# Block 0 of a retention-and-FFN kernel: fewer half steps, another order in the fifth visit, a step kept for chunk 8

## The chip, the cores and the metric

The kernel runs on one core of one Trainium2 chip. Its engines are named as the profile names them: PE (TensorE, matmuls; PEld is its weight load), DVE (VectorE), ACT (ScalarE), POOL (GpSimd) and SP (SyncE, which issues most transfers). The metric is the device time of one execution in microseconds (us); lower is better.

## The reference

Eight heads of retention over eight sequences of 576 tokens, and then a feed-forward layer with squared ReLU over all 4608 tokens:

```python
# q, k, v: (8, 8, 576, 64)
scores = (1 / sqrt(D)) * q @ k.T
ret = scores * Dmat            # Dmat[h, i, j] = gamma_h ** (i - j) for i >= j, else 0
attn = ret @ v
x = attn.transpose(0, 2, 1, 3).reshape(4608, 512)
h = np.maximum(x @ w_in, 0.0)  # w_in: (512, 2048)
out = h * h @ w_out            # w_out: (2048, 512)
```

## The kernel before

The retention runs in chunks of 128 tokens (five to a sequence, the last of 64). The feed-forward layer runs in blocks of 512 tokens, and each product of a block is a *step* on a list, which the loop over the chunks takes from to fill PE between the small matmuls of retention. Blocks 1 to 8 use products of sums and differences of quarter matrices (lines 595 and 866); block 0 uses plain products, because its weights are still being brought in.

The weights arrive as raw 64-bit words and are converted to float32 in 16 *pieces* for `w_in`, each by five DVE and two ACT operations. `round_parts` gives the six parts, and `w_in_parts` deals them out in order. `convert(n)` emits the next n of them:

```python
# lines 196 to 230, shortened
def fetch_w(j):
    if j < len(pieces) and wide:
        nc.sync.dma_start(raw_of(j)..., piece_src(j))            # L196
...
    def one():    nc.vector.tensor_scalar(exp, hi, ...)          # L210, waits for the raw piece
    def two():    nc.vector.tensor_scalar(bits, hi, ...)         # L214
    def beside():
        nc.scalar.activation(exp, exp, ...)                      # L218
        nc.scalar.activation(frac, lo, ...)                      # L219
    def three():  nc.vector.scalar_tensor_tensor(t, bits, ...)   # L222
    def four():   nc.vector.tensor_tensor(t, t, exp, ...)        # L225
    def five():   nc.vector.scalar_tensor_tensor(bits, hi, ...)  # L228
```

```python
    def w_in_parts():

        parts = [round_parts(j) for j in range(N_W1)] + [[None] * 2]
        for j in range(N_W1):
            one, two, beside, three, four, five = parts[j]
            if j <= N_HALF:
                yield from (one, two)
            yield beside
            if j >= N_HALF:
                yield from parts[j + 1][0:2]
            yield three
            yield four

            def last(five=five):
                five()
                n_made[0] += 1
                if n_next[0]:
                    fetch_raw(2)

            yield last
```

So from piece `N_HALF` on, the first two parts of the next piece come before the last three of a piece.

One piece's product for block 0 is `first_in(j)`: 512 tokens at once, or 256 of them (`halves`) when the block's other tokens aren't there yet. Its result is squared later, from a queue that the next calls empty:

```python
def first_in(j, halves=(0, 1)):
    assert n_made[0] > j
    ...
    for c in range(N_DM):
        nc.tensor.matmul(p..., lhsT=w[:, c, :], rhs=xT[0][:, c, lo * HT:hi * HT], ...)   # L559
    ...
    nc.scalar.activation(t, p, AF.Relu)                                                  # L564
    some(2)
    queue.append(lambda: nc.vector.tensor_tensor(t, t, t, op=ALU.mult))                  # L567
```

Of a chunk, `turn(i)` transposes k and q on PE (L387), copies kT on ACT (L393) and makes qT on DVE (L395, or L397 with the decay from chunk 4 on); `scores(i)` needs both (L415) and masks the result on DVE (L420 or L422). `retain_a` and `retain_c` add the chunk's own products and grow the state (L436, L439), `retain_b` adds the state's part (L471) and ends with a small ACT copy that serves as a fence for what follows on PE:

```python
    nc.scalar.copy(u_sb[...][:, 0:2, 0:1], xp[0][:, :, cs - CH:cs - CH + 1])             # L474
```

`retain_c` then copies the chunk's result to the block's xT on ACT (L493). The steps of block 0, and what takes them from chunk 4 on:

```python
    def block_steps(n):
        if n == 0:
            seconds = [(0, lambda j: (first_in(j, (1,)), first_in(j + 1, (1,))), j) for j in range(0, N_HALF, 2)]
            return seconds + [(0, first_in, j) for j in range(N_HALF, N_W1)]
        return [(n, ffn_in, n, mp, j) for mp in range(N_MP) for j in range(NP)]
...
    N_0 = N_W1 - N_HALF // 2
    PACE = (...)          # points (tokens, steps done) that the later visits aim at
...
    def ffn(i, half):

        gone[0] += chunks[max(0, min(i, N_CH - 1))][3] / 2
        if steps and steps[0][0] == 0:

            for f in (step, lambda: convert(6)) if half else (lambda: convert(6), step):
                f()
            if half and steps and steps[0][0] == 0:
                step()
                convert(6)
            return
        ...
```

The loop's visits; i counts from 0, `N_EARLY` is 4, so visit 4 is the fifth:

```python
    for i in range(N_CH + 1):
        if i <= N_EARLY:

            if i == 1:
                convert(2)
            elif i == 2:
                convert(5)
            if i >= 1:
                retain_a(i - 1)
                if i < 3:
                    warm(4, False)
                else:
                    convert(1)
                    first_in(2 * i - 5, (0,))
                    convert(5)
                retain_b(i - 1)
                if i < 3:
                    warm(4, False)
                retain_c(i - 1)
            convert((0, 1, 1, 0, 1)[i])
            if i == N_EARLY:
                fetch_raw(2)
                step()
            scores(i)
            if i == 2:
                convert(5)
                first_in(0, (0,))
            elif i == 3:
                convert(1)
                first_in(2, (0,))
                convert(5)
            elif i == N_EARLY:
                convert(5)
                step()
                convert(6)
            if i < N_EARLY:
                if i + 1 < N_EARLY:
                    scale_q(i + 1, nc.gpsimd)
                if i < 2:
                    warm(6, False)
                turn(i + 1)
        else:
            if i == N_EARLY + 1:
                gone[0] = TOK
            retain_a(i - 1)
            if i < N_CH:
                turn(i)
            ffn(i - 1, 0)
            retain_b(i - 1)
            if i < N_CH:
                scores(i)
            retain_c(i - 1)
            ffn(i - 1, 1)
        if i == 0:
            fetch_raw(2)
        if i + 3 < N_CH:
            load(i + 3)
        if 0 < i < N_EARLY:
            fetch_raw(1)
    assert n_next[0] == N_BLK
```

Of the kernel before, what the change touches and what calls it, by code (L numbers as in the profile page):

```python
# [40 lines left out]
def kernel(  # L41
# [87 lines left out]
    N_EARLY = TOK // C  # L129
# [27 lines left out]
    pieces = [(0, m, e) for m in range(N_M) for e in range(2)]  # L157
    pieces += [(1, mq + mh * N_MQ, e) for mq in range(N_MQ) for mh in range(2) for e in range(2)]
    N_W1 = N_DF
    N_HALF = 4  # L160
    stage = [W[5].rearrange("p (o s f) -> p o s f", o=4, s=NP),
             W[6][:, 0:3 * NP * 128].rearrange("p (o s f) -> p o s f", o=3, s=NP)]
    N_RAW = 6
# [30 lines left out]
    def fetch_w(j):  # L194
        if j < len(pieces) and wide:
            nc.sync.dma_start(raw_of(j).bitcast(I64).rearrange("p (c f) -> p c f", c=N_DM), piece_src(j))  # L196
# [88 lines left out]
    def fetch_raw(count):  # L285

        for _ in range(count):
            if n_raw[0] < min(N_W1, n_made[0] + N_RAW):
                fetch_w(n_raw[0])
                n_raw[0] += 1  # L290

    def w_in_parts():

        parts = [round_parts(j) for j in range(N_W1)] + [[None] * 2]
        for j in range(N_W1):
            one, two, beside, three, four, five = parts[j]
            if j <= N_HALF:
                yield from (one, two)
            yield beside  # L300
            if j >= N_HALF:
                yield from parts[j + 1][0:2]
            yield three
            yield four
# [9 lines that stand above are left out]
    w_in_steps = w_in_parts()  # L314

    def convert(count):
        for _ in range(count):
            f = next(w_in_steps, None)
            f and f()
# [39 lines left out]
    def rows(half, n=64):  # L359
        return slice(64 * half, 64 * half + n)  # L360
# [13 lines left out]
    def scale_q(i, engine):  # L374

        ci, t = chunks[i][1], loaded[i][0]
        engine.tensor_tensor(t, t, dv[:, :, NCH + ci:NCH + ci + 1].to_broadcast([C, H, D]), op=ALU.mult)

    def turn(i):

        cs, c0 = chunks[i][3], chunks[i][2]
        n_h = cs // CH
        p = ps_t.tile([128, 2, 512], F32, tag="t", name="t_ps").rearrange("p h (j d t) -> p h j d t", j=2, d=HP)
        for j in (1, 0):
            for hp in range(HP):
                for h in range(n_h):
                    nc.tensor.transpose(p[:, h, j, hp, :], loaded[i][j][rows(h), 2 * hp:2 * hp + 2, :],  # L387
                                        ident[rows(h), rows(h)])
        for j, name in ((1, "kT"), (0, "qT")):
            t = st[i][name] = work2.tile([128, HP, C], F32, tag=name, name=name) if j == 0 else work.tile([128, HP, C], F32, tag=name, name=name)  # L390
            to = t[:, :, :cs].rearrange("p d (h t) -> p h d t", h=n_h)
            if j:
                nc.scalar.copy(to, p[:, :n_h, j, :, :])  # L393
            elif i < N_EARLY:
                nc.vector.tensor_copy(to, p[:, :n_h, j, :, :])  # L395
            else:
                nc.vector.tensor_tensor(to, p[:, :n_h, j, :, :], dq[:, :, c0:c0 + cs].rearrange("p d (h t) -> p h d t", h=n_h),  # L397
                                        op=ALU.mult)
# [145 lines left out]
    def some(count=1):  # L544
        for f in queue[:count]:
            f and f()
        del queue[:count]

    def first_in(j, halves=(0, 1)):

        assert n_made[0] > j
        wi, m, e = pieces[j]
        mp, mm = divmod(m, 2)
        p = ps_f.tile([128, 2, HT], F32, tag="f", name="h_ps")
        w = w_in[mp][:, mm, 2 * e:2 * e + 2, :, :].rearrange("p s c f -> p (s c) f")
        lo, hi = halves[0], halves[-1] + 1
        p = p[:, lo:hi, :]
        for c in range(N_DM):
            nc.tensor.matmul(p.rearrange("p h t -> p (h t)"), lhsT=w[:, c, :], rhs=xT[0][:, c, lo * HT:hi * HT],  # L559
                             start=(c == 0), stop=(c == N_DM - 1))  # L560

        t = g_room[mp % 2][:, 3:7:3, mm, :] if e else g_room[mp % 2][:, 0:5:4, mm, :]
        t = t[:, lo:hi, :]
# [4 lines that stand above are left out]
        if mm and e and hi == 2:  # L568
            queue.append(lambda: [nc.sync.dma_start(
                g_dram[0, a:b, :, 2 * mp:2 * mp + 2, :].rearrange("s p m t -> p s (m t)"),  # L570
                g_room[mp % 2][:, a:b, :, :].rearrange("p s m t -> p s (m t)")) for a, b in QUARTERS])
        if j >= N_W1 - 4:

            sums_w.setdefault(0, sum_w_in(0)).pop(0)()
            if n_next[0] > 1:
                if 1 not in sums_x:
                    sums_x[1] = sum_x(1)
                sums_x[1].pop(0)()
# [73 lines left out]

    def block_steps(n):
        if n == 0:
            seconds = [(0, lambda j: (first_in(j, (1,)), first_in(j + 1, (1,))), j) for j in range(0, N_HALF, 2)]
            return seconds + [(0, first_in, j) for j in range(N_HALF, N_W1)]
        return [(n, ffn_in, n, mp, j) for mp in range(N_MP) for j in range(NP)]

    def step():
        n, f, *args = steps.pop(0)  # L660
        done[0] += 1
        f(*args)
# [3 lines left out]

    HALF = C // 2
    N_0 = N_W1 - N_HALF // 2
    PACE = ((4 * TOK + HALF // 4, N_0 + 2 * N_MP * NP - 2), (5 * TOK - HALF, N_0 + 3 * N_MP * NP - 2),  # L670
            (6 * TOK + HALF // 4, N_0 + 4 * N_MP * NP - 2), (8 * TOK + HALF // 4, N_0 + 6 * N_MP * NP - 2),
            (9 * TOK, N_0 + 7 * N_MP * NP - 2))
    done = [0]
# [30 lines left out]
    def warm(count, wide):  # L704
        t = ps_f.tile([128, 512], F32, tag="f", name="idle_ps")
        for _ in range(count):
            if wide:
                nc.tensor.matmul(t[:, 0:128], lhsT=idle, rhs=idle, start=True, stop=True)
            else:
                for b in range(2):  # L710
                    nc.tensor.matmul(t[rows(b), 0:64], lhsT=idle[rows(0), rows(b)], rhs=idle[rows(0), 0:64], start=True, stop=True,
                                     skip_group_check=True)
# [4 lines left out]
# [8 lines that stand above are left out]
                retain_a(i - 1)  # L725
                if i < 3:
                    warm(4, False)
                else:
                    convert(1)
                    first_in(2 * i - 5, (0,))  # L730
                    convert(5)
                retain_b(i - 1)
                if i < 3:
                    warm(4, False)
                retain_c(i - 1)
            convert((0, 1, 1, 0, 1)[i])
            if i == N_EARLY:
                fetch_raw(2)
                step()
            scores(i)  # L740
            if i == 2:
                convert(5)
# [3 lines that stand above are left out]
                first_in(2, (0,))  # L746
                convert(5)
            elif i == N_EARLY:
                convert(5)
                step()  # L750
                convert(6)
            if i < N_EARLY:
                if i + 1 < N_EARLY:
                    scale_q(i + 1, nc.gpsimd)
                if i < 2:
                    warm(6, False)
                turn(i + 1)
        else:
            if i == N_EARLY + 1:
                gone[0] = TOK  # L760
# [15 lines that stand above are left out]
# [239 lines left out]
```

## Time and profile before

| | before |
|---|---|
| device time, median of 3 runs | 993.59 us (993.35 to 995.42) |
| span of the profiled execution | 991.7 us |
| mean granted PE clock | 0.998 of full speed |
| DVE busy | 748.6 us (75%) |
| ACT busy | 190.4 us (19%) |
| transfers over the span | 221 GB/s |
| PE busy from 20 to 30, 30 to 40, 40 to 50 us | 7.83, 6.98, 9.32 us |
| PE busy from 50 to 100 us | 50.00 us |

The profile is one execution. An engine is busy while it works on an instruction; waiting is not busy. A matmul of float32 is recorded as two, so that `first_in` on half the tokens leaves 8 records of 128x256. A wait names the instruction that released it. An arrow in brackets after a row of the timeline shows how long the engine had been idle before it and who ended that. All the line numbers are those of the kernel before; in the changed kernel they are one higher from line 160 on and up to four higher near the end of the loop.

### The profile page before, as it was taken

To read this page: it belongs to the slowest core of one execution; us is meant where nothing else is said; L and a number is where in the kernel's file an instruction comes from. 1 tells how busy PE (TensorE), PEld (TensorE's weight loads), DVE (VectorE), ACT (ScalarE), POOL (GpSimd) and SP (SyncE) were. 2 spreads that over 40 slices of the span, in tenths; PEclk is the share of its full clock that TensorE was granted. 3 is DMA by queue.
4 is the path that set the end of the run, shared out by engine and by line. 5 is a ranking of instruction groups with operands and counts; after the bars stand their busy time and mean duration, and the time that the engine had idled before them with its cause. 6 is when DMAs were issued, how large, how long until landed. Compare 5 with 4: busy or idle time off the path is not lost.

```text
span 991.7 us, 24441 instructions
## 1 busy us (share of the span) xinstructions
PE 973.5 (98%) x10532; PEld 869.5 (88%) x10532; DVE 748.6 (75%) x1427; ACT 190.4 (19%) x462; POOL 81.6 (8%) x85
## 2 busy tenths in 40 slices
PE   7899999999999999999999999999999999999998
PEld 7655688888888888888888889999999999999998
DVE  4688696567878888897886777777777777777765
ACT  3444222222222222223221010000000000000000
POOL 3100011111111111111111000000000000000000
PEclk9999999999999999999999999999999999999999
DMA  9984657665696878769458999675673757556351
GB/s 205 250 239 143 174 172 208 162 175 176 187 311 199 223 234 260 224 209 283 142 212 297 404 389 348 235 283 163 230 268 148 265 197 270 192 213 216 126 212 44
DMA packets 187676, 220.40 MB, mean 222 GB/s; under 512 B 119216, under 2 KB 137648, under 8 KB 178608
## 3 DMA queue, kind: packets, MB, share of 16 engines
q1 hardware_dynamic: 185456, 218.31, 67.8%
q8 instruction: 83, 1.36, 0.6%
q10 hardware_dynamic: 2112, 0.52, 0.2%
q14 instruction: 25, 0.20, 0.1%
HBM read 129.41 MB, written 89.39 MB: 221 GB/s over the span
## 4 chain that ended last, share of the span: by engine, by line
PE 91%; DVE 5%; DMA 1%; SPq 1%; issue 1%; ACT 1%; DVEq 0%; ACTq 0%
PE o_b L866 17%; PE h_b L595 16%; PE o_c L866 11%; PE o_a L866 11%; PE h_a L595 10%; PE h_c L595 10%; PE h_ps L559 5%; PE x_ps L436 3%; PE t_ps L387 2%; PE sc_ps L415 2%; PE x_ps L471 2%; DVE room L602 1%; PE u_ps L439 1%; DMA w<-in_moe_w_in_dram 1%; DMA w<-in_moe_w_out_dram 0%
## 5 line engine op out<-in xcount | busy, mean ns | idle before, releaser
L595 PE MATMUL h_b<-room,w 128*128 128x256 f32 x736 | 177.2, 383 | 1.2 <-DVE room L520 0.9
L595 PEld LDWEIGHTS h_b<-room,w 128*128 128x128 f32 x736 | 137.2, 190 | 21.4 <-PE t_ps L387 1.1
L866 PE MATMUL o_b<-w,room 128*128 128x128 f32 x1168 | 144.5, 275 | 0.2 <-DVE room L817 0.2
L866 PEld LDWEIGHTS o_b<-w,room 128*128 128x128 f32 x1168 | 137.2, 192 | 0.5 <-DVE room L817 0.4
L866 PE MATMUL o_c<-w,room 128*128 128x128 f32 x1008 | 123.0, 275 | 0.0
L866 PEld LDWEIGHTS o_c<-w,room 128*128 128x128 f32 x1008 | 117.7, 192 | 0.0
L595 PE MATMUL h_c<-room,w 128*128 128x256 f32 x480 | 114.4, 381 | 0.0
L595 PE MATMUL h_a<-room,w 128*128 128x256 f32 x448 | 107.6, 383 | 0.0
L595 PEld LDWEIGHTS h_c<-room,w 128*128 128x128 f32 x480 | 90.4, 190 | 12.6
L595 PEld LDWEIGHTS h_a<-room,w 128*128 128x128 f32 x448 | 83.7, 190 | 11.8
L866 PE MATMUL o_a<-w,a 128*128 128x128 f32 x688 | 85.6, 275 | 0.0
L866 PEld LDWEIGHTS o_a<-w,a 128*128 128x128 f32 x688 | 81.2, 192 | 0.1
L612 POOL TENSOR_TENSOR room<-room 128x512 f32<-128x512 f32 x32 | 35.2, 1100 | 438.2 <-ACT room L611 370.6
L602 DVE SCALAR_TENSOR_TENSOR room<-room 128x512 f32<-128x512 f32 x96 | 68.1, 710 | 3.3
L880 ACT COPY r<-o_a 128x128 f32<-128x128 f32 x53 | 14.1, 266 | 271.7 <-PE o_a L866 241.2
L559 PE MATMUL h_ps<-room,w 128*128 128x512 f32 (+1 forms) x160 | 60.1, 526 | 2.5 <-DVE w L228 1.7
L614 DVE TENSOR_TENSOR room<-h_b,room 128x512 f32<-128x512 f32 x32 | 22.1, 690 | 46.9 <-PE h_b L595 46.9
L436 PEld LDWEIGHTS x_ps<-ret,v_ld 64*64 64x64 f32 x1152 | 40.4, 136 | 15.9 <-issue 11.7
L436 PE MATMUL x_ps<-ret,v_ld 64*64 64x64 f32 x1152 | 50.0, 226 | 3.5 <-ACT u_sb L474 3.4
L559 PEld LDWEIGHTS h_ps<-room,w 128*128 128x128 f32 x160 | 30.3, 196 | 24.6 <-issue 19.1
L424 POOL TENSOR_TENSOR v_ld<-v_ld,dv 128x512 f32<-128x512 f32 (+1 forms) x40 | 42.8, 1075 | 63.5 <-DMA v_ld<-in_v_dram 58.6
L876 DVE TENSOR_TENSOR small<-o_b,small 128x128 f32<-128x128 f32 x62 | 18.1, 292 | 38.4 <-PE o_b L866 38.4
(109 smaller groups left out, 1377.4 us busy)
## 6 DMA issues: line engine op xcount, KB each, us to landing
g_dram<-room SPq DMA_DIRECT2D x32, 1792.0 KB, 7.7
a<-g_dram SPq DMA_DIRECT2D x43, 1024.0 KB, 7.1
room<-g_dram SPq DMA_DIRECT2D x20, 1024.0 KB, 6.4
w<-w_dram SPq DMA_DIRECT2D x7, 1792.0 KB, 13.0
out_dram<-room SPq DMA_DIRECT2D x17, 512.0 KB, 3.4
w<-in_moe_w_in_dram SPq DMA_DIRECT2D x16, 512.0 KB, 6.1
w<-in_moe_w_out_dram SPq DMA_DIRECT2D x16, 512.0 KB, 4.1
v_ld<-in_v_dram SPq DMA_DIRECT2D x31, 256.0 KB, 4.4
```

The costliest lines, as they stand in the source:

```text
L387: nc.tensor.transpose(p[:, h, j, hp, :], loaded[i][j][rows(h), 2 * hp:2 * hp + 2, :], ident[rows(h), rows(h)])
L415: nc.tensor.matmul(sc[e][rows(h), hp, :], lhsT=kT[rows(e), hp, t], rhs=qT[rows(e), hp, t], start=True, stop=True, skip_group_check=True)
L424: nc.gpsimd.tensor_tensor(vs[:cs], vs[:cs], dv[:cs, :, ci:ci + 1].to_broadcast([cs, H, D]), op=ALU.mult)
L436: own.append(lambda hp=hp, e=e, b=b: nc.tensor.matmul(x_at(hp, b, h), lhsT=s["vs"][rows(h), 2 * hp + b, :], rhs=s["ret"][rows(h), e, hp, : ...
L471: nc.tensor.matmul(x_at(hp, b, h), lhsT=u[rows(e), hp, :], rhs=s["qT"][rows(e), hp, CH * h:CH * h + CH], start=clears(b, hp // 2), stop=Fa ...
L559: nc.tensor.matmul(p.rearrange("p h t -> p (h t)"), lhsT=w[:, c, :], rhs=xT[0][:, c, lo * HT:hi * HT], start=(c == 0), stop=(c == N_DM - 1))
L595: nc.tensor.matmul(p[:, mm, :], lhsT=w[:, c, :], rhs=xs[n][right][:, c, :], start=(j in OPENS and mm == 0 and c == 0), stop=(j in CLOSES a ...
L602: nc.vector.scalar_tensor_tensor(t, t, 0.0, t, op0=ALU.max, op1=ALU.mult)
L612: nc.gpsimd.tensor_tensor(g["A11"], g["A11"], g["A11"], op=ALU.mult)
L614: nc.vector.tensor_tensor(g["A22"], p, p15, op=ALU.add)
L866: nc.tensor.matmul(p, lhsT=s["lefts"][left][:, m, :], rhs=w_out[j][:, m, WO_SLOT[right], :], start=(i in OPENS and m == 0), stop=(i in CLO ...
L876: nc.vector.tensor_tensor(s["u2"], p, s["p1"], op=ALU.add)
```

## The change

The change touches block 0 only, while the weights of `w_in` arrive.

- `N_HALF` falls from 4 to 3: pieces 0 to 2 are done in two halves, piece 3 in one. The point from which the conversion deals parts of the next piece ahead stays at 4 (`N_ALONE`).
- The second halves become a step each instead of one step for two pieces, so block 0 has 16 steps and not 14.
- In visit 4 (the fifth), `turn(4)` moves from the end of visit 3 into the place between `retain_a` and `retain_b`. The conversion and the half product that stood there are gone, so no conversion stands in front of the fence at the end of `retain_b`; none stands between `retain_c` and `scores` either.
- `scores(4)` comes before the second halves, and two single steps with conversions follow it.
- With 16 steps, two in visit 4 and three in each of the next four, two steps are left for the visit of chunk 8, which had none of block 0 before.

The matmuls that are done are the same in sum. The whole diff:

```diff
--- before.py
+++ after.py
@@ -157,7 +157,8 @@
     pieces = [(0, m, e) for m in range(N_M) for e in range(2)]
     pieces += [(1, mq + mh * N_MQ, e) for mq in range(N_MQ) for mh in range(2) for e in range(2)]
     N_W1 = N_DF
-    N_HALF = 4
+    N_ALONE = 4
+    N_HALF = 3
     stage = [W[5].rearrange("p (o s f) -> p o s f", o=4, s=NP),
              W[6][:, 0:3 * NP * 128].rearrange("p (o s f) -> p o s f", o=3, s=NP)]
     N_RAW = 6
@@ -295,10 +296,10 @@
         parts = [round_parts(j) for j in range(N_W1)] + [[None] * 2]
         for j in range(N_W1):
             one, two, beside, three, four, five = parts[j]
-            if j <= N_HALF:
+            if j <= N_ALONE:
                 yield from (one, two)
             yield beside
-            if j >= N_HALF:
+            if j >= N_ALONE:
                 yield from parts[j + 1][0:2]
             yield three
             yield four
@@ -652,7 +653,7 @@
 
     def block_steps(n):
         if n == 0:
-            seconds = [(0, lambda j: (first_in(j, (1,)), first_in(j + 1, (1,))), j) for j in range(0, N_HALF, 2)]
+            seconds = [(0, first_in, j, (1,)) for j in range(N_HALF)]
             return seconds + [(0, first_in, j) for j in range(N_HALF, N_W1)]
         return [(n, ffn_in, n, mp, j) for mp in range(N_MP) for j in range(NP)]
 
@@ -666,7 +667,7 @@
 
 
     HALF = C // 2
-    N_0 = N_W1 - N_HALF // 2
+    N_0 = N_W1
     PACE = ((4 * TOK + HALF // 4, N_0 + 2 * N_MP * NP - 2), (5 * TOK - HALF, N_0 + 3 * N_MP * NP - 2),
             (6 * TOK + HALF // 4, N_0 + 4 * N_MP * NP - 2), (8 * TOK + HALF // 4, N_0 + 6 * N_MP * NP - 2),
             (9 * TOK, N_0 + 7 * N_MP * NP - 2))
@@ -725,18 +726,17 @@
                 retain_a(i - 1)
                 if i < 3:
                     warm(4, False)
+                elif i == N_EARLY:
+                    turn(i)
                 else:
                     convert(1)
-                    first_in(2 * i - 5, (0,))
+                    first_in(1, (0,))
                     convert(5)
                 retain_b(i - 1)
                 if i < 3:
                     warm(4, False)
                 retain_c(i - 1)
-            convert((0, 1, 1, 0, 1)[i])
-            if i == N_EARLY:
-                fetch_raw(2)
-                step()
+            convert((0, 1, 1, 0, 0)[i])
             scores(i)
             if i == 2:
                 convert(5)
@@ -746,15 +746,19 @@
                 first_in(2, (0,))
                 convert(5)
             elif i == N_EARLY:
-                convert(5)
-                step()
-                convert(6)
+                fetch_raw(2)
+                convert(1)
+                for _ in range(2):
+                    step()
+                    convert(5)
+                    convert(1)
             if i < N_EARLY:
                 if i + 1 < N_EARLY:
                     scale_q(i + 1, nc.gpsimd)
                 if i < 2:
                     warm(6, False)
-                turn(i + 1)
+                if i + 1 < N_EARLY:
+                    turn(i + 1)
         else:
             if i == N_EARLY + 1:
                 gone[0] = TOK
```

## The prediction

> **What bounds the kernel now.** First the page's busy table and slices, for the whole:
>
> ```profile
> PE 973.5 (98%) x10532; PEld 869.5 (88%) x10532; DVE 748.6 (75%) x1427; ACT 190.4 (19%) x462; POOL 81.6 (8%) x85
> ```
>
> TensorE (PE) is busy in 973.5 of 991.7 us, so 18 us at most can come from its idle time, and the diff neither adds nor removes matmul work. The change can only move idle time, and time at a lowered clock, in block 0. So next I read PE's list of waits for the first 115 us, and then the timeline around the largest.
>
> ```profile
> PE x_ps L436 <- ACT u_sb L474: 2.1, 2, 1.8
> PE h_ps L559 <- DVE w L228: 1.7, 3, 0.6
> PE h_ps L559 <- ACT room L493: 0.9, 2, 0.7
> PE sc_ps L415 <- DVE qT L397: 0.3, 1, 0.3
> ```
>
> The columns are total us, times, longest. The first line's 1.8 us is the fence of visit 4 (the fifth): PE waits for the small ACT copy L474. The timeline of PE, with start and duration first and the idle time in brackets, shows it and what follows it:
>
> ```profile
> 40.00 0.27 PE L436 MATMUL x_ps<-ret,v_ld 64*64 64x64 f32 x2 [1.80 <-ACT u_sb L474]
> ...
> 41.37 5.17 PE L559 MATMUL h_ps<-room,w 128*128 128x256 f32 x16 [0.68 <-ACT room L493]
> ...
> 47.08 3.72 PE L559 MATMUL h_ps<-room,w 128*128 128x256 f32 x16
> ...
> 55.45 0.69 PE L415 MATMUL sc_ps<-qT,kT 64*64 64x64 f32 x32
> ```
>
> The same 16 records (two half pieces) take 5.17 us and then 3.72 us: the first pair ran at a lowered clock. The windows view confirms it, its columns being PE, PEld, DVE, ACT and POOL busy, granted clock, DMA share, GB/s:
>
> ```profile
> 37.50:40.90 3.40, 1.39 (x65) 1.11 (x64) 1.43 (x4) 1.76 (x5) 0.00 (x0) 1.00 1.06 208
> 40.90:44.30 3.40, 2.93 (x7) 2.39 (x8) 0.00 (x0) 0.69 (x2) 1.06 (x1) 0.50 0.95 288
> ```
>
> Then what held ACT's copy. The timeline of DVE shows two long waits for raw weights, and the operation that scores of chunk 5 need:
>
> ```profile
> 37.90 0.43 DVE L210 TENSOR_SCALAR w<-w 128x512 uint32<-128x512 uint32 x1 [2.44 <-DMA w<-in_moe_w_in_dram]
> 38.24 0.42 DVE L214 TENSOR_SCALAR w<-w 128x512 uint32<-128x512 uint32 x1
> 38.57 0.42 DVE L397 TENSOR_TENSOR qT<-t_ps,dq 128x256 f32<-128x256 f32 x1
> 38.91 0.42 DVE L567 TENSOR_TENSOR room<-room 128x256 f32<-128x256 f32 x1
> 44.59 0.43 DVE L210 TENSOR_SCALAR w<-w 128x512 uint32<-128x512 uint32 x1 [5.26 <-DMA w<-in_moe_w_in_dram]
> ...
> 54.71 0.68 DVE L397 TENSOR_TENSOR qT<-t_ps,dq 128x512 f32<-128x512 f32 x1
> 55.31 0.42 DVE L210 TENSOR_SCALAR w<-w 128x512 uint32<-128x512 uint32 x1
> ```
>
> Raw piece 4 lands at 37.9 and raw piece 5 at 44.6. ACT's two conversion operations wait for DVE's L210 at 37.90, and the fence copy stands behind them on ACT. That is the 1.8 us. From 44.59 DVE runs without a gap until chunk 5's qT at 54.71, and PE asks for that qT at 55.45, just after it is ready.
>
> **What the Trainium skill says.** "TensorE: Matmul & The Clock Gate", Part 1: The HAM clock gate, says that PE is gated to half its clock after an idle window of about 3.4 us, in windows that run freely. The trace agrees in size: 3.4 us at clock 0.50 after a window with 1.39 us of PE work; so full idleness was not needed. "Perfetto Trace Analysis", Tensor Engine Instruction, says that ACT and DVE are strict FIFO; the L397 above that stands behind a waiting L210 agrees. The same page, Identifying the Most-Contended Engine, warns that PE's busy share doesn't measure the distance to its peak; the 2.93 busy us in a half-clock window show why I look at the clock too.
>
> **The change part by part.** A half piece costs 1.83 us at full clock (from 47.08 to 50.73 for two), a full piece 3.63 (51.38 to 55.01), so one full piece instead of two halves saves nothing. The parts differ in when things stand on each queue.
>
> *Removed in visit 4:* the conversion in front of the fence, and piece 3's first half (35.60 to 37.50). *Moved:* turn(4) comes after retain_a(3), the scores of chunk 4 before all second halves. *Left out there:* one of three whole conversions, and the work of pieces 3 and 4, which PE formerly did before scores(5).
>
> Fence: up to 33.65 nothing differs. retain_a(3) 0.70, turn(4) 0.64, retain_b(3) 0.69 and retain_c(3) 0.69, by the same rows of before, with two short waits on ACT copies, end at about 36.4; the 1.8 us wait is gone. But chunk 4's qT still stands behind piece 4's L210 and L214, issued on DVE in visit 3, and the SP order up to there is unchanged, so the raw piece still lands at 37.9: qT ends at 38.99, and scores(4) start at 39.05. PE idles some 2.6 us there.
>
> PE then has only scores(4) 0.61, three second halves 5.48, turn(5) 0.65 and retain_b(4) 0.44: 7.2 us, to about 46.2, before scores(5). Those need chunk 5's qT. DVE's queue before it now holds: from 44.59 (raw piece 5, again unchanged) the five operations of a conversion step to 47.32 as before; one square, 0.34; raw piece 6's two operations and piece 5's three, 2.72 (48.59 to 51.31 before); so qT starts at 50.38 and ends about 51.06. Raw piece 6 was issued at 39.67 and took 7.7 us in before, landing at 47.4, just in time. So scores(5) start at **51.1 instead of 55.45**, after some 5 us of PE idling.
>
> Balance at that point: 4.35 us earlier, but pieces 3 and 4 now lie ahead instead of behind, where before had done all four halves of them: 2 x 3.63 = 7.26 us. **Net loss 2.9 us.** The same from idle time: before loses 0.62 + 1.80 + 0.68 and 1.45 to the clock (5.10 less 3.65) between 33.65 and 55.45, 4.55 us; after loses 17.45 less 9.9 of work, 7.5 us.
>
> Clock: before paid 1.45 there. After, a stretch of 3 to 5 us without matmuls ends at 51.1, longer than the one that cost before its clock. A half clock for 3.4 us costs 1.7 us once PE is loaded again; I count **1.5**, between before's 1.45 and that, as windows may fall otherwise. A drop at 39 to 43 is hidden in the wait.
>
> From 51.1 to the end of visit 8 PE should be full, as it was from 47 to 104 before: DVE is one conversion further behind by visit but PE two pieces.
>
> Visit 9, chunk 8: two pieces remain (14 and 15) and stand in its two slots. Before, PE waited 0.30 us for qT of chunk 9 and then, in visit 10, for qT of chunk 10, which had five operations of block 1 in front of it:
>
> ```profile
> 122.85 0.69 PE L415 MATMUL sc_ps<-qT,kT 64*64 64x64 f32 x32 [1.48 <-DVE qT L397]
> ```
>
> After, chunk 10's qT stands behind one sum of block 1 only, and PE has three products between turn and scores: both waits go, **1.8 us gained**; block 1's second product may wait for its sum behind that qT, an estimate of 0.3 us from 0.6 us per operation there. Net -1.5.
>
> Sum: 2.9 + 1.5 - 1.5 = **+2.9**, from 993.6 to **996.5 us**. The pace afterwards aims at the same points, its count of steps raised by the same two, so the rest of the run should be alike.
>
> **Rivals.**
> 1. *The fence bounds the visit.* Then its 1.80, the 0.68 behind it and the 1.45 of clock are all saved and chunk 8's 1.5 too: some 988 to 989 us. For it: the wait list's first row and the chain, which goes through that fence. Against: the raw transfers at 37.9 and 44.6 stand behind every qT, and PE has little to do meanwhile.
> 2. *The clock doesn't drop, or a window falls well.* Then about 995.
> 3. *Raw piece 6 lands later or DVE becomes the bound through visits 5 to 8.* 7.7 us of flight ends only 0.3 us before it is needed; each us late is a us on scores(5). Then 998 to 1000. Against: DVE's busy share in 60 to 100 us was about 83% with PE full.
> 4. *Everything is hidden anyway.* With PE full for the remaining 900 us nothing absorbs a delay, so I give this little.
>
> **Range and chances.** 996.5, from 993.0 (half the conversion wait absorbed, no clock loss) to 1000.0 (two clock drops or a late transfer). 2% is 20 us, more than block 0's visit 4 can move: faster 0.005, same 0.985, slower 0.01.
>
> **What would show it.** Right: no L474 wait near 40; PE idle before scores(4) until 39.0, waiting for qT; a wait of 3 to 5 us before scores(5), ending at 51, for qT; half clock for some 3 us thereafter; no wait for qT at chunks 9 and 10. Wrong: scores(5) starting near 47, or raw pieces landing at other times, since all the times rest on those two landings.

## The result, and the profile after

The changed kernel takes 998.82 us (median of 4 runs, 998.12 to 1000.34); the kernel before, beside it, 994.2 us. The ratio is 1.0048, with a 95% interval of 1.003 to 1.0065: slower by some 4.6 us, within 2%. The profiled span grew from 991.7 to 996.4 us. Line numbers of the changed kernel are one higher here: L398 is the qT of L397, L475 the fence copy, L211 a conversion's first operation.

PE's waits of the changed kernel between 30 and 130 us (total us, times, longest):

```profile
PE sc_ps L416 <- DVE qT L398: 5.7, 2, 3.1
PE x_ps L437 <- ACT u_sb L475: 1.5, 3, 0.9
PE h_ps L560 <- DVE w L229: 0.5, 1, 0.5
```

The fence wait of 1.8 us near 40 is gone, though another fence wait of 0.9 us has come, and PE waits 5.7 us for qT, in two waits. The timeline of PE shows both, and the products behind them:

```profile
39.41 1.12 PE L416 MATMUL sc_ps<-qT,kT 64*64 64x64 f32 x16 [3.10 <-DVE qT L398]
40.46 5.54 PE L560 MATMUL h_ps<-room,w 128*128 128x256 f32 x16
...
51.55 1.13 PE L416 MATMUL sc_ps<-qT,kT 64*64 64x64 f32 x32 [2.59 <-DVE qT L398]
53.60 1.12 PE L437 MATMUL x_ps<-ret,v_ld 64*64 64x64 f32 x16 [0.92 <-ACT u_sb L475]
54.65 8.70 PE L560 MATMUL h_ps<-room,w 128*128 128x512 f32 x16
63.91 0.46 PE L388 MATMUL t_ps<-ident,k_ld 64*128 64x64 f32 x8
```

The scores of chunk 5 start at 51.55 (55.45 before). The two full pieces behind them, 3 and 4, take 8.70 us; before, two took 7.13 (the row at 56.53 further down). DVE's timeline says what these scores waited for:

```profile
38.26 0.43 DVE L211 TENSOR_SCALAR w<-w 128x512 uint32<-128x512 uint32 x1 [3.07 <-DMA w<-in_moe_w_in_dram]
...
45.02 0.43 DVE L211 TENSOR_SCALAR w<-w 128x512 uint32<-128x512 uint32 x1 [3.42 <-DMA w<-in_moe_w_in_dram]
...
50.81 0.68 DVE L398 TENSOR_TENSOR qT<-t_ps,dq 128x512 f32<-128x512 f32 x1
```

Raw pieces 4 and 5 land at 38.3 and 45.0 and DVE then runs without a gap to chunk 5's qT. The windows of the same profile show the clock (columns: PE, PEld, DVE, ACT, POOL busy, granted clock, DMA share, GB/s):

```profile
51.00:54.40 3.40, 1.93 (x47) 1.77 (x48) 3.33 (x7) 1.59 (x4) 0.00 (x0) 0.50 0.70 205
54.40:57.60 3.20, 3.20 (x11) 1.53 (x8) 3.13 (x8) 0.37 (x1) 0.00 (x0) 0.50 1.19 235
```

This half clock lasts from 51.0 to 57.8, 6.8 us: twice the 3.4 us that before had at 40.9 to 44.3. An earlier one, from 37.4 to 44.2, lies over the wait before the scores of chunk 4 and the two half pieces behind them (5.54 us).

### The profile page after: what moved, and what is told of

The parts are those of the page before. It is cut to its first block, busy times and chain, and to the rows that moved or that the text cites. A ratio compares the mean times of both kernels' runs of the same rounds, so it can differ in the third digit from the quotient of the medians. Undisturbed runs are those within 1.5% of the kernel's fastest.

```text
span 996.4 us, 24418 instructions
## 1 busy us (share of the span) xinstructions
PE 975.9 (98%) x10524; PEld 869.9 (87%) x10524; DVE 747.7 (75%) x1426; ACT 190.7 (19%) x461; POOL 83.9 (8%) x85
## 4 chain that ended last, share of the span: by engine, by line
PE 92%; DVE 4%; ACT 1%; DMA 1%; issue 1%; SPq 1%; DVEq 0%; ACTq 0%
PE o_b L870 17%; PE h_b L596 16%; PE o_c L870 11%; PE o_a L870 11%; PE h_c L596 11%; PE h_a L596 11%; PE h_ps L560 5%; PE x_ps L437 3%; PE t_ps L388 2%; PE x_ps L472 2%; PE sc_ps L416 2%; PE u_ps L440 1%; DMA w<-in_moe_w_in_dram 1%; PE idle_ps L712 0%; DVE room L603 0%
## 5 line engine op out<-in xcount | busy, mean ns | idle before, releaser
L560 PE MATMUL h_ps<-room,w 128*128 128x512 f32 (+1 forms) x152 | 62.1, 560 | 1.2 <-DVE w L229 1.0
L425 POOL TENSOR_TENSOR v_ld<-v_ld,dv 128x512 f32<-128x512 f32 (+1 forms) x40 | 44.2, 1108 | 69.2 <-DMA v_ld<-in_v_dram 47.6
L880 DVE TENSOR_TENSOR small<-o_b,small 128x128 f32<-128x128 f32 x62 | 18.1, 292 | 38.3 <-PE o_b L870 38.3
```

Of the source, the lines that this page charges most:

```text
L425: nc.gpsimd.tensor_tensor(vs[:cs], vs[:cs], dv[:cs, :, ci:ci + 1].to_broadcast([cs, H, D]), op=ALU.mult)
L880: nc.vector.tensor_tensor(s["u2"], p, s["p1"], op=ALU.add)
```

## The experiments

Each was timed beside the kernel before on the same chip. Its medians were 994.9 to 995.4 us there and 994.2 beside the changed kernel, so medians of two experiments can differ by about 1 us for that reason alone, and the ratio to before is the better measure. "Changed" is the kernel after, and scores(5) are the scores of chunk 5. The texts before each run call experiment 4 qt5_first, 5 qt5_fence and 11 both_qt. Diffs with comments in them are shortened.

**1. The fence alone.** In the kernel before, visit 4's conversion goes behind the fence.

```diff
-   convert(1); first_in(3, (0,)); convert(5)        # visit 4, before retain_b
+   first_in(3, (0,))
-   convert(1)                                       # visit 4, after retain_c
+   convert(7)
```

> The kernel before, with the conversion of piece 4 in visit 4 put behind the fence (nothing else moved). Theory (chunk 5's qT, behind three conversions on DVE that start when raw piece 5 lands near 44.6 us, sets when scores of chunk 5 start): the 1.8 us fence wait near 40 goes, but scores(5) still start near 55.4 and PE waits some 2 to 3 us for qT just before them; time within 1.5 us of before (about 994). Rival (the fence bounds the visit): the 1.8 us, the 0.7 us behind it and the 1.4 us of half clock are saved, about 990.5.

Measured: 996.14 us, ratio to before 1.0014 (1.0 to 1.0029). PE's timeline of this run:

```profile
39.30 0.27 PE L436 MATMUL x_ps<-ret,v_ld 64*64 64x64 f32 x2 [0.28 <-ACT u_sb L474]
...
56.67 0.80 PE L415 MATMUL sc_ps<-qT,kT 64*64 64x64 f32 x32 [1.99 <-DVE qT L397]
```

The fence wait fell from 1.80 to 0.28 us, and 1.99 us appeared before the scores of chunk 5. The half clock moved with the idle time, from 40.9 to 44.3 in before to 57.2 to 60.5 here, so that was not saved either. The fence wait was the longest in the visit and removing it gained nothing: some 16 us later PE can't pass chunk 5's qT in either kernel. Raw piece 5 landed at 45.81 in this profile, 1.2 us later than in before's, and the scores start as much later. The distance from this landing to scores(5) is 10.86 us in all three profiles with the old order: before (44.59 to 55.45), this one (45.81 to 56.67) and that of experiment 2 (45.02 to 55.88), while the fence wait is 1.80, 0.28 and 0.83 us. The fence, the longest wait that the change removed, was not the bound.

**2. The kept steps alone.** In the kernel before, chunks 6 and 7 take two steps, so that two are left for chunk 8.

```diff
-            if half and steps and steps[0][0] == 0:
+            if half and steps and steps[0][0] == 0 and i not in (N_EARLY + 2, N_EARLY + 3):
```

> The kernel before, with two full steps of block 0 kept for chunk 8 (the visits of chunks 6 and 7 take two steps and not three). Theory: the waits of 0.30 us (chunk 9's qT) and 1.48 us (chunk 10's qT) go and about 0.3 us comes back, so about 1.5 us faster than before, 992.7. Rival (the wait only moves to a later visit of block 1): the same as before, 994.2.

Measured: 992.88 us, ratio 0.9986 (0.997 to 1.0003). No wait of PE for another engine is listed between 100 and 130 us, where before had 1.8 us for qT. The interval includes 1. In its profile no half clock fell at 41 to 44, as before's did, but one at 22.5 to 25.9. So the waits are shown to be gone, and the gain in time is only likely.

**3. The changed kernel without the kept steps.**

```diff
                 step()
                 convert(6)
+                if i in (N_EARLY + 2, N_EARLY + 3):
+                    step()
+                    convert(6)
```

> The changed kernel without the two steps kept for chunk 8 (the visits of chunks 6 and 7 take four steps each). Theory: the waits for qT of chunks 9 and 10 come back, about 1.5 us slower than the changed kernel, 1000.3. Rival (the kept steps pay nothing here): 998.8.

Measured: 1000.71 us, ratio to before 1.006 (1.0045 to 1.0075), against 1.0048 of the changed kernel. Its waits between 100 and 130 us:

```profile
PE sc_ps L416 <- DVE qT L398: 1.8, 2, 1.5
```

The same 1.8 us as before are back. So the kept steps remove these waits in both kernels. In time they are worth 1.2 us here by the ratios, 1.9 by the medians; the intervals overlap, so the size is not shown.

**4. Chunk 5's qT first, fence as it was.** In the changed kernel, the last seven parts of visit 4 move to just behind turn(5).

```diff
-                for _ in range(2):
-                    step()
-                    convert(5)
-                    convert(1)
+                step()
+                convert(5)
+                step()
...
             if i < N_CH:
                 turn(i)
+            if i == N_EARLY + 1:
+                convert(7)
             ffn(i - 1, 0)
```

> The changed kernel with the last seven conversion parts of visit 4 moved to just behind turn(5), so that chunk 5's qT stands in front of piece 5's conversion on DVE, all conversions of visit 5 still in front of its fence. Theory (qT behind the conversion makes the wait, but the fence of visit 5 is a second bound at nearly the same time): scores(5) start near 49.3 and not 51.6, but PE then waits for the fence copy until about 53.5, and the time stays within 1 us of the changed kernel, 998.8. Rival (qT is the only bound there): 2.5 us of waiting and the half clock go, 993 to 995.

Measured: 998.47 us, ratio 1.0039 (1.0019 to 1.0058), as the changed kernel. PE:

```profile
50.82 0.69 PE L416 MATMUL sc_ps<-qT,kT 64*64 64x64 f32 x32 [1.20 <-DVE qT L398]
55.60 1.12 PE L437 MATMUL x_ps<-ret,v_ld 64*64 64x64 f32 x16 [4.09 <-ACT u_sb L475]
```

The wait for qT shrinks and the fence's grows to 4.09 us. The fence copy stood on ACT behind the conversions of pieces 5 to 7. Raw piece 5 landed at 47.01 here, 2.0 us later than in the changed kernel's profile, and this was the slowest of the four runs (1001.44), so the times are to be read from that landing: chunk 4's own products start 8.59 us behind it, in the changed kernel 8.58 (45.02 to 53.60). The move freed the scores and left the fence where it was.

**5. Both bounds at once.** As 4, but the seven parts and the conversion of visit 5's first half (six parts) go behind the scores of chunk 5 and the products of chunk 4.

```diff
+   # visit 5, behind turn(5): step(); retain_b(4); scores(5); retain_c(4)
+   convert(13)
```

> As qt5_first, but the moved conversion and that of the visit's first half stand behind the fence and the scores of chunk 5. Theory (both bounds gone): scores(5) near 49.3, no fence wait, clock full after 51, so pieces 3 and 4 take 7.3 us and not 8.7; about 5.5 us faster than the changed kernel, 993.3. Rival (PE then runs into unfinished conversions, because they start later): a new wait of PE for DVE at pieces 5 to 7, gain under 2 us, 997 or more.

Measured: 1000.16 us, ratio 1.0048 (1.0033 to 1.0063): no gain, and my theory's 5.5 us missed. Yet in visit 5 what it said happened, a little later:

```profile
50.38 0.65 PE L416 MATMUL sc_ps<-qT,kT 64*64 64x64 f32 x32
...
51.55 7.13 PE L560 MATMUL h_ps<-room,w 128*128 128x512 f32 x16
```

The scores started without a wait, and the two pieces ran at full clock. The waits between 56 and 72 us show where the gain went:

```profile
PE x_ps L437 <- ACT u_sb L475: 1.3, 1, 1.3
PE x_ps L472 <- ACT u_sb L446: 1.0, 1, 1.0
PE sc_ps L416 <- DVE qT L398: 1.0, 1, 1.0
```

Visit 6 now has 3.3 us of waits for the same three things, with half clock from 66 to 73 after them. The 13 parts that I moved stood in front of *chunk 6's* qT, kT and fence. The rival had the time right, but not the place: PE waited in visit 6, not at pieces 5 to 7.

**6. The same with fewer parts.** Only the count differs from 5: seven parts come later.

```diff
-                convert(13)
+                convert(6)
```

> As qt5_fence, but 6 parts of conversion and not 13 behind the scores of chunk 5, so that 7 parts fewer stand in front of chunk 6's qT on DVE; the rest follows later, as each visit deals out the same number. Theory (qt5_fence won 4.7 us by chunk 6's turn and lost it in visit 6, where chunk 6's qT and fence stood behind the conversions that it had moved there): the waits of 3.3 us in visit 6 and the half clock behind them go, and what qt5_fence was to bring comes, 993 to 995, so 4 to 6 us under the changed kernel. Rival (DVE has no room for them later either): the waits come back in visit 7 or 8, 998 or more.

Measured: 992.08 us (6 runs, 991.0 to 993.01), ratio 0.9965 (0.9949 to 0.9981). No wait of PE for another engine is listed from 56 to 75 us, and PE's timeline runs through:

```profile
48.22 0.69 PE L416 MATMUL sc_ps<-qT,kT 64*64 64x64 f32 x32 [1.17 <-DVE qT L398]
48.73 0.64 PE L437 MATMUL x_ps<-ret,v_ld 64*64 64x64 f32 x16
49.30 7.13 PE L560 MATMUL h_ps<-room,w 128*128 128x512 f32 x16
...
61.71 0.69 PE L416 MATMUL sc_ps<-qT,kT 64*64 64x64 f32 x32
```

Some 8 us under 5, by the place of seven parts on two queues. (Raw piece 5 landed at 44.41 here and at 45.96 in 5's profile; that accounts for 1.5 us between the two profiles at most.) It also shows that the changed kernel's other parts can beat the kernel before once the conversions stand elsewhere.

**7. The conversion in front of visit 5's fence alone.** The changed kernel with that one `convert(6)` behind `retain_c(4)`.

> The changed kernel with the one conversion in front of visit 5's fence put behind the scores of chunk 5 and chunk 4's own products. Theory (the fence copy stands on ACT behind the conversion of piece 7, whose first operation waits on DVE behind chunk 5's qT): the 0.9 us wait for the fence copy near 53 goes, the half clock stays; 0.5 to 1.5 us faster than the changed kernel, 997.3 to 998.3. Rival (the later conversion gives it back at chunk 6's qT, as when more conversions were moved): no difference.

Measured: 997.81 us, ratio 1.0021 (0.9994 to 1.0048). The 0.9 us wait went, the half clock stayed, from 50.3 to 57.2:

```profile
52.64 1.07 PE L437 MATMUL x_ps<-ret,v_ld 64*64 64x64 f32 x16
```

From the landing of raw piece 5 to the next turn PE took 17.89 us (45.20 to 63.09), 1.0 less than in the changed kernel (45.02 to 63.91). The medians also differ by 1.0 us and the ratios by 2.7, though the intervals overlap.

**8. Chunk 4's qT alone.** In the changed kernel, piece 4's first two parts move behind scores(4): `convert(5)` to `convert(3)` in visit 3, `convert(1)` to `convert(3)` in visit 4.

> The changed kernel with chunk 4's qT alone put in front of the two operations that wait for raw piece 4; those of piece 5 stay in front of chunk 5's qT. Theory (scores(5), bound by raw piece 5 and two conversion steps behind it, are the bound; the wait before scores(4) is only a part of the same waiting): scores(4) start near 36.5 and not 39.4, the wait before scores(5) grows by what was saved, to 5 us or more, scores(5) stay near 51.5; within 1.5 us of the changed kernel, 998.8. Rival (the two waits add up): 2.5 us faster, 996.3.

Measured: 998.72 us, ratio 1.0033 (1.0005 to 1.0061), the same as the changed kernel. PE:

```profile
51.46 0.95 PE L416 MATMUL sc_ps<-qT,kT 64*64 64x64 f32 x32 [4.48 <-DVE qT L398]
```

The wait of scores(4) for qT shrank from 3.10 to 0.19 us (0.70 us more stood idle inside these scores, with no releaser in the profile), and that before scores(5) grew from 2.59 to 4.48; they still start at 51.5. The first wait was part of the second. Scores(5) start 6.53 or 6.54 us behind the landing of raw piece 5 in all six profiles that have the changed kernel's conversions between the two: the changed kernel (45.02 to 51.55), 3, 7, 8, 9 and 10.

**9 and 10. Is the half clock a cost of its own?** Small matmuls on an idle tile, whose results nobody reads, were put into the waits: in 9, `warm(16)` between retain_b(4) and scores(5); in 10, `warm(22)` before scores(4), `warm(36)` before and `warm(8)` behind scores(5).

> The changed kernel with 16 pairs of small matmuls on an idle tile between retain_b(4) and scores(5), where PE waits 2.6 us for chunk 5's qT; added work, no other order. Theory (the half clock after 51 us is a cost of its own, set by the lack of matmuls before it): scores(5) still start near 51.6, but the clock stays full, pieces 3 and 4 take 7.3 us and not 8.7, scores and chunk 4's own products lose 0.5 us less; about 2 us faster than the changed kernel, 996.8. Rival (the slow stretch comes from something else than idleness, or the added work delays the scores): 998.8 or slower.

> The changed kernel with small matmuls on an idle tile in all three long waits: 22 pairs before the scores of chunk 4, 36 before those of chunk 5, 8 behind them, where the fence wait is. Order and conversions as in the changed kernel. Theory (the time that PE runs at half clock from 51 to 58 us is a cost of its own, set by too few matmuls in the window before): no half clock in 34 to 60 us, scores(5) at the same 51.5, pieces 3 and 4 in 7.3 us and not 8.7 to 9.2; 2.5 to 3.5 us faster than the changed kernel, 995.3 to 996.3, the waits for qT left as they are. Rival (the half clock is no loss, or the added matmuls delay the path): 998.8 or more.

Measured: 998.68 us for 9 (ratio 1.0035, 1.0018 to 1.0052) and 998.02 us for 10 (1.0018, 0.9985 to 1.0051). By the medians that is 0.1 and 0.8 us under the changed kernel, by the ratios 1.3 and 3.0, with intervals that overlap. In 9 the fill ended at 49.1 and the clock still fell near 52. In 10 the drop at 38 and that at 51 went, but 3.4 us of half clock came at 55.3:

```profile
55.52 8.73 PE L560 MATMUL h_ps<-room,w 128*128 128x512 f32 x16
```

The two pieces were as slow as in the changed kernel. So part of the drop was moved, not removed, and the test of the clock's price is inconclusive. It shows something else: the scores before them ran at full clock (0.69 us, not 1.13), and chunk 4's own products still started 2.07 us behind them (52.78 to 54.85; in the changed kernel 2.05), because they waited for the fence copy (0.44 us for L475).

**11 and 12. Every qT in front.** 11 joins 8 with what 5 and 6 showed (a count of tokens that the edit also adjusts is left out here):

```diff
-    N_ALONE = 4
+    N_ALONE = 5
-    convert(5)                            # visit 3, behind first_in(2)
+    convert(3)
     fetch_raw(2)                          # visit 4, behind scores(4)
-    convert(1)
-    for _ in range(2):
-        step(); convert(5); convert(1)
+    step(); convert(6); step()
     # visit 5: step() without a conversion up to scores(5) and retain_c(4), then
+    step(); convert(6); step(); convert(12)
```

> The changed kernel with every qT in front of the conversion that waits for a raw piece: piece 4's first two parts move out of visit 3 to behind scores(4), the next piece is dealt ahead from piece 5 on only, one conversion between chunk 4's scores and chunk 5's turn, the conversions of visit 5 behind its fence. Theory (PE's waits from 36 to 54 us are all DVE and ACT queues behind raw pieces 4 and 5): no wait before scores(4) and scores(5), which start near 36.5 and 44, retain_a(5) near 52 to 54 and not 63; about 10 us faster than the changed kernel, 988 to 990, and below the kernel before. Rival (the landing of raw pieces bounds whatever the order): PE waits for piece 4 or 5 instead, 993 or more.

Measured: 989.85 us, ratio to before 0.9949 (0.9935 to 0.9964). Scores(5) started at 45.42, 1.4 us later than expected and after a wait of 0.94 us for qT; from 20 to 120 us the clock stayed full. One wait for qT was left in visit 6:

```profile
60.30 0.69 PE L416 MATMUL sc_ps<-qT,kT 64*64 64x64 f32 x32 [1.38 <-DVE qT L398]
```

12 only puts the conversion before the step in visit 5, `convert(6); step(); convert(6); step(); convert(6)`:

> As both_qt, but in visit 5 the first conversion stands in front of the step and not behind it, so that ACT's conversion doesn't wait behind that step's ReLU. Theory (DVE was idle 3.5 us there for ACT, and so chunk 6's qT came 1.4 us too late): that wait goes, about 1.4 us faster than both_qt, 988.5. Rival (another wait takes its place, DVE being full): 989.8.

Measured: 988.65 us, ratio 0.9931 (0.9903 to 0.9958). PE's waits of 12 from 33 to 135 us are all of these:

```profile
PE h_ps L560 <- DVE w L229: 1.4, 1, 1.4
PE sc_ps L416 <- DVE qT L398: 0.4, 1, 0.4
PE x_ps L437 <- ACT u_sb L475: 0.3, 1, 0.3
```

The first of them ends at 32.55, ahead of the stretch in question. Chunk 6's qT is no longer waited for; 12 against 11 is in the expected direction, but their intervals overlap. Both beat both kernels. DVE's timeline of 12 shows the raw pieces:

```profile
40.25 0.43 DVE L211 TENSOR_SCALAR w<-w 128x512 uint32<-128x512 uint32 x1 [1.16 <-DMA w<-in_moe_w_in_dram]
...
44.43 0.68 DVE L398 TENSOR_TENSOR qT<-t_ps,dq 128x512 f32<-128x512 f32 x1
...
47.60 0.43 DVE L211 TENSOR_SCALAR w<-w 128x512 uint32<-128x512 uint32 x1 [0.98 <-DMA w<-in_moe_w_in_dram]
```

Pieces 4 and 5 landed *later* than in before (37.9 and 44.6), and the kernel is 6.7 us faster (988.65 against 995.35 us beside it): chunk 5's qT no longer stands behind piece 5. The landing of raw pieces was a bound only for what stood behind it on DVE.

## Why the prediction was right, point by point

996.5 us had been predicted, with 993.0 to 1000.0; 998.82 was measured. The difference was to be +2.9 us and is +4.6 by the medians, +4.7 in the span. The mechanism was right; one bound was overlooked and the clock was priced too low. For the clock, these are the rows of before that follow scores(5), which start at 55.45:

```profile
55.96 0.64 PE L436 MATMUL x_ps<-ret,v_ld 64*64 64x64 f32 x16
56.53 7.13 PE L559 MATMUL h_ps<-room,w 128*128 128x512 f32 x16
...
64.22 0.46 PE L387 MATMUL t_ps<-ident,k_ld 64*128 64x64 f32 x8
```

- *The fence goes and gains nothing.* Right; experiment 1 shows it in the kernel before.
- *Scores(4) wait until 39.05 for qT behind raw piece 4.* 39.41, as that piece landed 0.4 us later. The wait was 3.10 us and not 2.6. Experiment 8 shows that the wait had no price of its own.
- *Scores(5) start at 51.1, bound by raw piece 5 and two conversion steps.* 51.55, with the raw piece 0.4 us later. From landing to scores it said 6.5 us, and six profiles have 6.53 or 6.54: this is the step on which the argument rests, and it held. PE's wait there was 2.59 us and not some 5, below the 3 named as a sign, because the half clock of 37.4 to 44.2 filled part of it; as predicted, that drop was hidden. That both landings came within 0.5 us of before's was luck: the prediction took them as fixed because the order of transfers was, but they vary by over 2 us from profile to profile.
- *Net loss at that point 2.9 us.* 55.45 less 51.55 is 3.90 earlier, 7.26 us of work more ahead: 3.4 us, of which 0.4 is the later landing.
- *The clock, 1.5 us.* This term was too small, and the fence of visit 5 is missing beside it. From scores(5) to the next turn, with two pieces between, before took 64.22 - 55.45 = 8.77 us, the changed kernel 63.91 - 51.55 = 12.36: 3.6 us lost. From scores(5) to chunk 4's own products it took 2.05 us and not 0.51. These 1.5 us belong to the fence of visit 5, which the prediction had overlooked: experiments 4 and 10 show that the fence copy sets that start, whether the scores run at half clock or not. The other 2.1 us are the half clock: the same products took 1.05 us to the next start and not 0.57, and the two pieces 8.63 and not 7.06. The half clock lasted 6.8 us and not 3.4; PE was busy in only 1.93 of the first 3.4 us. I had taken the length of a drop from before, where the work behind it was dense.
- *Chunk 8, -1.5 us.* -1.8 in the profile: the two waits for qT went and no wait took their place. Experiments 2 and 3 show the same waits go and come back; in time they give 1.4 and 1.2 us by the ratios, within the noise.
- *Sum.* 3.4 + 1.5 + 2.1 - 1.8 = 5.2 us, against 4.7 in the span; where the last half us lies I did not follow.

Of the rivals, the first (the fence bounds the visit) fell in experiment 1. The second (no loss of clock) did not come about. The third did not occur in the changed kernel: raw piece 6 was not waited for, and PE was busy throughout from 58 to 104 us. The waits in visit 6 of experiment 5 look like it, but experiment 6 shows that the order made them, and not too much work on DVE. The fourth, that all is hidden, fell with the +4.6 us.

## What to carry to other kernels

A wait at the head of the list may cost nothing: ask what the engine would wait for next, and remove that wait alone, in the old kernel, before building an order around it. Where one in-order queue carries both short operations that another engine needs soon and long chains that wait for transfers, put the short ones ahead of the first operation that can wait, and count the parts in front of the *next* short one too; seven parts' place was worth 8 us here. Work that fills a wait has to be there when the wait comes: in the kernel before, piece 3's first half and piece 4 were done ahead of scores(5), and the change left PE to wait 5.7 us there.

## What the runs showed of the hardware

The half clock came without full idleness: in before, after 3.4 us with 1.39 us of PE work (37.50 to 40.90). It lasted 3.4 us there, 6.8 in the changed kernel and 10.2 in experiment 4 (52.0 to 62.2). How much work ends it does not follow from PE's busy time alone: in before a stretch with 2.93 us busy of 3.4 was the last one, in the changed kernel one with 1.93 was not, but neither was one with 2.91 in experiment 3 (38.24 to 41.65) nor one with 3.25 in experiment 4 (55.43 to 58.85).

Raw piece 4 landed anywhere from 37.05 (experiment 6) to 39.73 us (experiment 5) with the same order of transfers ahead of it, so that single profiles of this stage differ by over 1 us, as the whole change's terms do. Times counted from a landing agree far better.
